# Sixth score buffer, a smaller pool of transposed weights, and another order of the last transposes in a top-k attention + MLP kernel

## The chip, the cores and the metric

The kernel runs on one core of a Trainium2 chip. The metric is the device time in microseconds (us) of one execution. A core has five engines that run their own instruction streams side by side: PE (matrix products), ACT (activation functions and copies), DVE (vector operations), POOL (vector operations too) and SP (here it only issues DMA transfers). Matrix products land in PSUM; the other engines work on SBUF and can read PSUM, POOL excepted in this kernel. Engines wait for each other through counting semaphores.

## The reference

Attention over 8 batches and 8 heads, 576 positions, head size 64, in which each query keeps only its 32 largest scores, followed by an MLP on the concatenated heads:

```python
scores = scale * q @ k.T
kth    = np.partition(scores, -32)[..., -32]      # the 32nd largest of each row
attn   = softmax(where(scores >= kth, scores, -1e9))
x      = (attn @ v) with the heads side by side    # 4608 x 512
h      = x @ w_in                                  # 4608 x 2048
out    = (maximum(h, 0) + alpha * minimum(h, 0)) @ w_out
```

The kernel folds the MLP's negative half into a linear product: with g = relu(h), the output is g @ ((1 - alpha) w_out) + x @ (w_in @ (alpha w_out)).

## The kernel before

Two heads form a pair, and the work is cut into 144 *duos*, 18 a batch. A duo is 128 query rows of both heads of a pair (or, for the 64 rows left over, the remainders of two pairs): two row blocks of 128 by 576 scores. D is the last duo, 143.

The main loop (`for n in range(ND)`) goes through 144 slots, and in each slot several duos are in work, each at another stage. In slot n:

- PE multiplies queries and keys of duo n+1 into PSUM (`st_qk`, tile `ps_sc`; there is one such PSUM tile), after waiting until the scores before were copied out.
- ACT counts for duo n-2 how many scores lie above an estimated threshold (`st_count`, tile `sg`, a sign with an accumulator), takes exp of the scores of duo n-4 (`st_exp`, tile `w`), writes its 0/1 mask with the final threshold (`st_cut`, tile `f`, two row blocks), and last copies the scores of duo n+1 from PSUM to SBUF (`st_exit`, tile `s_sb`). Every few slots it also copies transposed queries and keys (`qkT`) or output rows (`o_sb`).
- DVE takes the eight largest of each of six groups of every row of duo n (MAX8 from `s_sb`), folds them every second slot into a threshold estimate `p` that ACT's count of the next slots needs, picks the final threshold, takes MAX8 of `y`, and applies relu to MLP products (`gT`).
- POOL multiplies scores by signs (`st_y`, tile `y`) for duo n-2 and exp by mask (`w<-w,f`) for duo n-4.
- SP issues a DMA transpose of the masked weights of duo n-4 (`st_wT`, tile `wT`); PE multiplies `wT` with v (`st_av`, tile `xo`) in slot d+8 for duos d below 13 and in slot d+7 for the others. DVE normalizes every second duo to `x`, SP transposes x to `xT` (`st_xT`), and PE runs the MLP on it (`ph`: first layer, `pz`: second layer).
- Where PE would have nothing to do, products of a constant tile (`rest`) are put in.

The order on each engine is the order of the calls: the class `Ordered` keeps every engine's program order, apart from a group of small DVE operations. SP's queue is in order too: loads of q, k and v, transposes of `wT`, `x` and of the weights, copies into `kd`, and most output stores are issued in the order in which they are written, and a transfer that waits for its data holds those behind it.

Tiles come from pools with a fixed number of buffers. A new tile of a pool reuses the buffer that is oldest, and its first writer waits for the last reader of the tile that was there. In this program the wait stands also where reader and writer are on the same engine: each `st_exit` carries a wait for PE (the product) and one for ACT's own count (the last reader of the buffer). The pools of the change: `s` (5 buffers of 4608 bytes a partition, tile `s_sb`), tag `wT` of the pool `three` (4 buffers of 2560 bytes, given by `bufs=4`; the pool's own number is 3), and `qk` (6 buffers of 4608 bytes, tile `qkT`).

After the loop comes the *drain*, written out by hand: the last duos' counts, masks and products. For D-3 and D-2 `st_cut` makes the mask on ACT and POOL as before; for D-1 and D `st_mask` does it on DVE. The weights of D are transposed by PE (`turn_w`) and copied to SBUF by DVE and ACT (`turned`); those of the others by SP. `normed(D-4)` gives the `x` whose transpose feeds the last MLP block but one, `normed(D-2)` the last.

Of the kernel before, what the change touches and what calls it, by code (L numbers as in the profile page):

```python
# [9 lines left out]
BF16 = mybir.dt.bfloat16  # L10
# [49 lines left out]
def fast_path(tc, q, k, v, moe_w_in, moe_w_out, moe_alpha, out, flag):  # L60
    nc = tc.nc
    B, H, S, D = q.shape
# [26 lines left out]
    ND = len(duos)  # L89
# [3 lines left out]
    with ExitStack() as ctx:  # L93
        pool = lambda name, bufs, **kw: ctx.enter_context(tc.tile_pool(name=name, bufs=bufs, **kw))
# [1 line left out]
        stg = pool("stg", 3)  # L96
        io = pool("io", 2)
        qk_p = pool("qk", 2 * KPB - 2)
        s_p = pool("s", 5)
        two = pool("two", 2)  # L100
        three = pool("three", 3)
        gp = pool("gp", 4)
# [14 lines left out]
        qkT, v1 = {}, {}  # L117
# [114 lines left out]
        T = {}  # L232
# [162 lines left out]
        def st_cut(n):  # L395
            w, s = ws[n % 4][:, :, 0:S], T.pop(("s", n))
            f = two.tile([128, 2, S], mybir.dt.uint8, name="f", tag="sg", bufs=3)
            for i in range(2):
                ACT.activation(f[:, i, :], s[:, i, :], AF.Sign, bias=KT[:, 2 * n + i:2 * n + i + 1])
            POOL.tensor_tensor(w, w, f.bitcast(mybir.dt.float8e4), ALU.mult)  # L400
            st_wT(n)

        def st_wT(n):
            w = ws[n % 4]
            wt = three.tile([128, 10, 128], BF16, name="wT", tag="wT", bufs=4)
            SP.dma_start_transpose(wt, w.rearrange("p a b -> p (a b)"))
            T["wt", n] = wt

# [141 lines left out]
        def ready():  # L550
            k = 0
            while lin_done and k < len(oq) and oq[k][0]["done"] >= oq[k][1]:
                k += 1
            return k
# [16 lines left out]
        def o_pe():  # L571
            if ready() and len(stores) < (1 if now[0] < ND else 2):
                oq.pop(0)[2]()
                return True
# [160 lines left out]
        for n in range(ND):  # L735
# [33 lines left out]
            for m in duos_at("cut", n):  # L769
                st_cut(m)  # L770
# [26 lines left out]
        def st_mask(d):  # L797
            w, s_ = ws[d % 4], T.pop(("s", d))
            kt = KT[:, 2 * d:2 * d + 2]
            for i in range(2):  # L800
                DVE.scalar_tensor_tensor(out=w[:, i, 0:S], in0=s_[:, i, :], scalar=kt[:, i:i + 1],
                                         in1=w[:, i, 0:S], op0=ALU.is_ge, op1=ALU.mult)
            if d < D:
                st_wT(d)
# [6 lines left out]
            return ps  # L811

        def turned(d, ps):
            wt = T["wt", d] = three.tile([128, 10, 128], BF16, name="wT", tag="wT", bufs=4)
            DVE.tensor_copy(wt[:, 0:5, :], ps[0])
            ACT.copy(wt[:, 5:10, :], ps[1])

# [11 lines left out]
        D = ND - 1  # L829
# [18 lines left out]
        st_y(D)  # L848
        st_exp(D - 3)
        st_cut(D - 3)  # L850
        st_exp(D - 2)
        row(D - 1, 0)
# [10 lines left out]
        row(D, 0)  # L863
        row(D, 1)
        st_cut(D - 2)
        picked(D // 2)
        normed(D - 4)
# [7 lines left out]
        h_relu(ACT)  # L875
        st_mask(D - 1)
        st_mask(D)
        o_pe()
        o_pe()
        o_act()  # L880
# [4 lines left out]
        ps = turn_w(D)  # L885
        st_av(D - 3)
        turned(D, ps)
        h_pe(2)
        h_relu(ACT)
# [263 lines left out]
@with_exitstack  # L1153
def kernel(
    ctx: ExitStack,
    tc: tile.TileContext,
    q: bass.AP,
    k: bass.AP,
    v: bass.AP,
    moe_w_in: bass.AP,  # L1160
    moe_w_out: bass.AP,
    moe_alpha: bass.AP,
    out: bass.AP,
):
    nc = tc.nc
    keep = ctx.enter_context(tc.tile_pool(name="keep", bufs=1))
    flag = keep.tile([1, 1], I32, name="flag")
    fast_path(tc, q, k, v, moe_w_in, moe_w_out, moe_alpha, out, flag)
    redo = nc.values_load(flag, min_val=0, max_val=1)
    with tc.If(redo > 0):  # L1170
        general_path(tc, q, k, v, moe_w_in, moe_w_out, moe_alpha, out)
# [30 lines left out]
```

In the profile nearly all operations stand under L32, the line of the helper in `Ordered` that records them; tile names tell them apart.

## Time and profile before

| | |
|---|---|
| median of 3 runs | 824.95 us (823.41 to 827.95) |
| profiled execution | 827.92 us, span 826.0 us |
| clock of TensorE granted, mean | 0.988 |
| instructions | 17830 |
| busy PE / DVE / ACT / POOL | 738.5 / 757.0 / 778.8 / 715.6 us |
| share of the chain that ended last | ACT 47%, PE 35%, issue 9%, DVE 4% |

The span is the time from the first to the last instruction. Busy times are unions of instruction times on one engine, so two instructions that overlap count once. A row of a timeline gives start, length, engine, operation, output and input tiles, shapes and a count; in square brackets stands how long the engine was idle before, and what ended that. A row of the waits gives who waited for whom, the total in us, how often, and the longest. In a row of groups the part behind the second bar is idle time just before the instructions of the group. "SPq" is SP issuing a transfer; the time to landing runs from issue to the last byte.

### The profile page before, as it was taken

Reading aid. Unit: us, or ns where it says so; the run is one execution under the profiler, and the core shown is the slowest. Engines: PE = TensorE matmul, PEld = TensorE weight load, DVE = VectorE, ACT = ScalarE, POOL = GpSimd, SP = SyncE. Lnnn points to the kernel's source line nnn. Section 1 sums busy time; section 2 is a strip of 40 time slices with the busy share of each in tenths; the row PEclk is TensorE's granted clock in tenths of the full one; section 3 lists DMA queues with packets and bytes.
Section 4 is the critical chain, followed back from the end, with each engine's and each line's share of the span. In section 5 each row is a group of like instructions: output and inputs, shape, how many; then the busy total and the mean of one; then the engine's idle time right before and its main releaser. Section 6 shows DMA issues by size and latency. Waiting matters only on the chain.

```text
span 826.0 us, 17830 instructions
## 1 busy us (share of the span) xinstructions
PE 738.5 (89%) x5375; PEld 423.8 (51%) x5448; DVE 757.0 (92%) x3470; ACT 778.8 (94%) x1265; POOL 715.6 (87%) x565
## 2 busy tenths in 40 slices
PE   8878999989889988989989999898979999999876
PEld 5333455545545554555545554555545555556553
DVE  4999999999999999999999999999999999999841
ACT  5999999999999999999999999999999999999941
POOL 2898899999998999999999899999999988988930
PEclk9999899999999999999999999999999999999989
DMA  7789996555566565655676565666665564544441
GB/s 156 190 171 184 163 159 112 111 117 115 121 119 123 112 126 120 129 113 110 128 121 120 121 124 122 106 123 117 119 141 110 123 134 79 98 97 100 83 81 37
DMA packets 342327, 99.90 MB, mean 121 GB/s; under 512 B 336128, under 2 KB 336400, under 8 KB 342224
## 3 DMA queue, kind: packets, MB, share of 16 engines
q1 hardware_dynamic: 338928, 91.18, 57.0%
q0 software_dynamic: 1952, 7.09, 3.6%
q8 instruction: 45, 0.74, 0.4%
q10 hardware_dynamic: 1344, 0.43, 0.2%
q14 instruction: 58, 0.48, 0.2%
HBM read 36.71 MB, written 9.44 MB: 56 GB/s over the span
## 4 chain that ended last, share of the span: by engine, by line
ACT 47%; PE 35%; issue 9%; DVE 4%; POOL 2%; DMA 2%; SPq 1%; ACTq 0%; POOLq 0%; DVEq 0%
ACT f L32 14%; ACT sg L32 13%; PE ps_sc L32 12%; ACT s_sb L32 11%; ACT w L32 7%; PE pz L32 6%; PE ph L32 6%; PE xo L32 5%; PE rest L32 2%; PE tps L32 2%; DVE small L32 1%; PE plin L32 1%; ACT qkT L32 1%; SPq L32 1%; POOL w L32 1%
## 5 line engine op out<-in xcount | busy, mean ns | idle before, releaser
L32 POOL TENSOR_TENSOR y<-s_sb,sg 128x576 f32<-128x576 f32 x288 | 362.2, 1278 | 24.3 <-ACT sg L32 24.1
L32 POOL TENSOR_TENSOR w<-w,f 128x1152 bf16<-128x1152 bf16 x142 | 317.8, 2239 | 51.8 <-ACT f L32 47.3
L32 DVE MAX8 up<-s_sb 128x8 f32<-128x96 f32 x864 | 212.2, 246 | 18.0 <-ACT s_sb L32 17.5
L32 ACT ACTIVATE sg<-s_sb,p 128x576 bf16<-128x576 f32 x288 | 220.7, 770 | 2.1 <-DVE p L32 2.0
L32 DVE MAX8 p<-y 128x8 f32<-128x576 f32 x288 | 215.1, 748 | 7.2 <-POOL y L32 7.0
L32 DVE MAX8 small<-s_sb 128x8 f32<-128x96 f32 x864 | 216.2, 250 | 0.0
L32 PE MATMUL ps_sc<-qkT 64*128 64x512 f32 (+2 forms) x768 | 184.5, 570 | 26.0 <-ACT s_sb L32 25.1
L32 ACT ACTIVATE f<-s_sb,KZ 128x576 uint8<-128x576 f32 x284 | 203.0, 763 | 0.0
L32 ACT COPY s_sb<-ps_sc 128x1152 f32<-128x1152 f32 x144 | 161.1, 1118 | 9.5 <-PE ps_sc L32 5.1
L32 ACT ACTIVATE w<-s_sb 128x1152 bf16<-128x1152 f32 x144 | 166.2, 1154 | 0.0
L32 PE MATMUL ph<-xT,w_in_b 128*128 128x256 bf16 (+1 forms) x1472 | 151.2, 251 | 13.8 <-DMA xT<-x 7.2
L32 PEld LDWEIGHTS <-w_in_b 128*128 128x128 bf16 x1472 | 121.2, 99 | 56.8 <-issue 12.5
L32 PE MATMUL pz<-w_out_b,gT 128*128 128x512 bf16 x545 | 142.1, 379 | 8.9 <-issue 6.0
L32 PE MATMUL xo<-v,wT 128*128 128x65 bf16 (+3 forms) x1600 | 126.5, 198 | 0.6 <-DVE x L32 0.6
L32 PEld LDWEIGHTS <-wT 128*128 128x128 bf16 (+3 forms) x1600 | 97.7, 99 | 29.1 <-issue 0.8
L32 DVE TENSOR_SCALAR gT<-ph 128x512 bf16<-128x512 f32 x134 | 90.3, 674 | 8.3 <-PE ph L32 8.1
L32 PEld LDWEIGHTS ps_sc<-qkT 64*128 64x128 f32 (+1 forms) x768 | 55.7, 169 | 70.9 <-ACT s_sb L32 39.7
L32 PEld LDWEIGHTS ps_sc<-kd,qkT 128*128 128x128 f32 x256 | 38.3, 188 | 97.8 <-issue 94.8
L32 PEld LDWEIGHTS <-gT 128*128 128x128 bf16 x576 | 54.5, 98 | 59.0 <-issue 4.4
L32 PE MATMUL ps_sc<-kd,qkT 128*128 128x128 f32 x256 | 62.8, 327 | 0.0
L32 PE MATMUL rest<-idle 128*128 128x512 bf16 x200 | 52.2, 387 | 6.9 <-DVE gT L32 4.8
L32 ACT ACTIVATION_READ_ACCUMULATOR sg<-s_sb,p 128x1 f32 x288 | 54.8, 190 | 0.0
(67 smaller groups left out, 569.7 us busy)
## 6 DMA issues: line engine op xcount, KB each, us to landing
k_st<-in_k_dram SPq DMA_DIRECT2D x64, 128.0 KB, 2.9
v_st<-in_v_dram SPq DMA_DIRECT2D x64, 128.0 KB, 2.8
q_st<-in_q_dram SPq DMA_DIRECT2D x62, 128.0 KB, 2.7
out_dram<-o_sb SPq DMA_DIRECT2D x29, 256.0 KB, 2.5
w_st<-in_moe_w_out_dram POOLq DMA_DIRECT2D x4, 1024.0 KB, 6.7
wT<-w SPq DMA_TRANSPOSE x143, 3.5
w_in_b<-in_moe_w_in_dram POOLq DMA_DIRECT2D x4, 512.0 KB, 6.0
k_st<-in_k_dram SPq DMA_DIRECT2D x32, 32.0 KB, 2.8
```

The source lines that it names most:

```text
L32: ins = self.tc.keep_in_program_order(f(*a, **kw))
```

## The change

- The pool of scores has six buffers instead of five.
- The tag `wT` has three buffers instead of four.
- The transposed weights of the last duo, D, lie in a buffer of the pool of keys and queries instead of one of `wT`.
- `st_cut` of duo D-2 no longer issues the transpose of its weights; the drain issues it after `st_mask(D)`. On SP's queue it thereby stands behind the transpose of the x of D-4 and that of the weights of D-1, where it stood ahead of both.

The order of instructions on PE, ACT, DVE and POOL is the same as before.

```diff
-        s_p = pool("s", 5)
+        s_p = pool("s", 6)
...
         def st_cut(n):
...
             POOL.tensor_tensor(w, w, f.bitcast(mybir.dt.float8e4), ALU.mult)
-            st_wT(n)
+            if n < ND - 3:
+                st_wT(n)

         def st_wT(n):
             w = ws[n % 4]
-            wt = three.tile([128, 10, 128], BF16, name="wT", tag="wT", bufs=4)
+            wt = three.tile([128, 10, 128], BF16, name="wT", tag="wT")
             SP.dma_start_transpose(wt, w.rearrange("p a b -> p (a b)"))
...
         def turned(d, ps):
-            wt = T["wt", d] = three.tile([128, 10, 128], BF16, name="wT", tag="wT", bufs=4)
+            wt = T["wt", d] = qk_p.tile([128, 10, 128], BF16, name="wT", tag="qkT")
...
         st_mask(D - 1)
         st_mask(D)
+        st_wT(D - 2)
         o_pe()
```

## The prediction

> **What bounds the kernel now.** I read the busy shares first, then the stages.
>
> ```profile
> PE 738.5 (89%) x5375; PEld 423.8 (51%) x5448; DVE 757.0 (92%) x3470; ACT 778.8 (94%) x1265; POOL 715.6 (87%) x565
> ```
>
> ACT is the busiest engine. The table by stage (length, then busy us and instructions of PE, weight loads, DVE, ACT, POOL; clock; DMA) says where.
>
> ```profile
> 20.00:100.00 80.00, 66.74 (x360) 30.21 (x358) 75.24 (x332) 78.05 (x131) 72.12 (x65) 0.94 0.87 181
> 100.00:200.00 100.00, 92.43 (x642) 52.10 (x652) 94.57 (x439) 99.40 (x162) 91.97 (x69) 1.00 0.64 120
> 200.00:600.00 400.00, 360.94 (x2615) 207.66 (x2654) 389.44 (x1811) 397.43 (x641) 371.63 (x278) 1.00 0.62 121
> 600.00:700.00 100.00, 92.52 (x688) 54.17 (x697) 96.05 (x438) 97.14 (x157) 89.58 (x67) 1.00 0.60 118
> 700.00:775.00 75.00, 72.06 (x629) 43.31 (x638) 72.34 (x336) 74.00 (x121) 68.78 (x49) 1.00 0.46 90
> 775.00:826.00 51.00, 36.33 (x361) 25.12 (x365) 20.41 (x58) 21.26 (x37) 16.97 (x15) 0.90 0.35 68
> ```
>
> Through the loop of slots ACT is occupied 99.4% of the time, so ACT sets the period; DVE follows at 97.4%, two points behind. In the drain (after 775) no engine is full: there a chain of waits sets the end.
>
> **The sixth score buffer.** ACT's groups of 200 to 600 us (busy, mean ns | idle before):
>
> ```profile
> L32 ACT ACTIVATE f<-s_sb,KZ 128x576 uint8<-128x576 f32 x152 | 108.6, 763 | 0.0
> L32 ACT ACTIVATE w<-s_sb 128x1152 bf16<-128x1152 f32 x76 | 87.7, 1154 | 0.0
> L32 ACT COPY s_sb<-ps_sc 128x1152 f32<-128x1152 f32 x75 | 83.9, 1119 | 2.6 <-PE ps_sc L32 0.2
> ```
>
> Only the copy that brings scores out of PSUM has idle time before it: 2.6 us, of which PE explains 0.2; the other 2.4 over 75 copies is 0.032 us each. The timeline (start, length) shows its neighbours:
>
> ```profile
> 402.98 1.43 ACT L32 ACTIVATE f<-s_sb,KZ 128x576 uint8<-128x576 f32 x2
> 404.43 1.12 ACT L32 COPY s_sb<-ps_sc 128x1152 f32<-128x1152 f32 x1
> ...
> 770.12 0.19 ACT L32 ACTIVATION_READ_ACCUMULATOR sg<-s_sb,p 128x1 f32 x1
> 770.21 0.56 ACT L32 COPY o_sb<-pz 128x512 f32<-128x512 f32 x1
> ```
>
> Two masks `f` of 0.763 take 1.43, so they overlap by 0.096; and o_sb's copy, also out of PSUM, starts 0.10 before its predecessor (770.31) ends. The score copy alone starts 0.02 to 0.03 after `f` ends (404.41). With five buffers the copy of duo n+1 overwrites the scores of duo n-4, whose last reader is exactly the `f` ahead of it, and the program waits for that `f` by ACT's own count. With six it waits for the `f` of the slot before, five us old. I take the gap for that wait: each copy can start 0.032 + 0.096 = 0.128 us sooner. There are 75 copies in the 400 us, one every 5.33, so 19 in each 100 us and 14 in the 75; in the first stage, whose slots are longer, I put 13. So ACT could give back 1.7 + 2.4 + 9.6 + 2.4 + 1.8 = 17.9 us; nothing excludes 0 at the other end (the first rival).
>
> ACT is not alone, so I look at what is late next. Waits in 20:100, then 100:200, 200:600, 600:700 and 700:775 (total us, times, longest):
>
> ```profile
> DVE p L32 <- POOL y L32: 3.7, 8, 0.9
> DVE up L32 <- ACT s_sb L32: 1.0, 3, 0.3
> ...
> DVE up L32 <- ACT s_sb L32: 3.7, 6, 1.1
> ...
> DVE up L32 <- ACT s_sb L32: 6.9, 15, 0.7
> DVE p L32 <- POOL y L32: 0.7, 2, 0.3
> ...
> DVE gT L32 <- PE ph L32: 2.5, 4, 1.0
> ACT sg L32 <- DVE p L32: 1.4, 1, 1.4
> ...
> DVE up L32 <- ACT s_sb L32: 2.0, 4, 0.6
> ```
>
> Between 200 and 600 DVE waits 6.9 us for ACT's copy and 0.7 for POOL's products: 7.6, after which DVE is the bound. So 9.6 is cut to at most 7.6; I take 6.0 (6.9 less about one, since long and short slots alternate and ACT in turn needs DVE's thresholds). In 20:100 and 100:200 DVE's waits of 4.7 and more leave room: I take 1.4 of 1.7 and 2.0 of 2.4. In 600:700 DVE waits for PE, and ACT for DVE, never DVE for ACT: 0.5 of 2.4. In 700:775 1.5 of 1.8. Loop: 1.4 + 2.0 + 6.0 + 0.5 + 1.5 = 11.4, at most 1.7 + 2.4 + 7.6 + 2.4 + 1.8 = 15.9.
>
> The Trainium skill speaks against this in "VectorE: DVE Perf Modes", section "The DRAIN you can't avoid": for that engine it says of a wait between consecutive operations that "the semaphore costs nothing extra here". By it, carried over to ACT, the loop's term would be 0. The page measures another engine, and the copies above contradict it for ACT by 0.128 us each, unless something else makes that gap.
>
> **Three buffers for wT instead of four.** SP's transpose of duo d must now wait for the product with v of duo d-3, not d-4. Before duo 13 that product comes a slot later than the transpose:
>
> ```profile
> 86.66 1.75 SPq L32 DMA_TRANSPOSE wT<-w  x1
> 95.52 1.80 SPq L32 DMA_DIRECT2D q_st<-in_q_dram  x3
> ...
> 88.12 1.09 PE L32 MATMUL xo<-v,wT 128*128 128x65 bf16 x10
> 102.66 0.60 PE L32 MATMUL tps<-ident_f,q_st 128*128 128x128 f32 x4
> ...
> q_st<-in_q_dram SPq DMA_DIRECT2D x62, 128.0 KB, 2.7
> ```
>
> This is the worst of them: issued at 86.66, now held until 89.21, 2.55 later. Behind it SP is busy without a break, so the queries issued at 95.52 to 97.32 slip by 2.55 to 99.9 at most. They are used at 102.66, 2.8 after their last issue, where these transfers take 2.7 to land by their median (last row): cost 0, at most 0.5. If that cover were gone, the transposes of queries and then the next scores would wait up to 2.55 once. From duo 16 on the product with v is done before the transpose everywhere; the closest:
>
> ```profile
> 683.42 1.33 SPq L32 DMA_TRANSPOSE wT<-w  x1
> 681.65 0.78 PE L32 MATMUL xo<-v,wT 128*128 128x65 bf16 x10
> ```
>
> done 682.43, needed 683.42: 0.98 to spare. The last duo's wT in a buffer of keys and queries waits only for score products that ended slots before: 0.
>
> **The drain's order.** The transposes of D-2 move on SP's queue behind xT of D-4 and behind wT of D-1.
>
> ```profile
> 787.58 0.42 DVE L32 TENSOR_TENSOR x<-xo,KZ 128x256 bf16<-128x256 f32 x1
> 788.08 4.85 DVE L32 SCALAR_TENSOR_TENSOR w<-s_sb,KZ,w 128x576 bf16<-128x576 f32 x4
> ...
> 775.51 1.33 SPq L32 DMA_TRANSPOSE wT<-w  x1
> 776.90 1.38 SPq L32 DMA_TRANSPOSE xT<-x  x1
> ...
> 787.95 3.65 SPq L32 DMA_TRANSPOSE wT<-w  x2
> 791.66 1.99 SPq L32 DMA_TRANSPOSE xT<-x  x1
> ...
> 796.88 3.60 PE L32 MATMUL ph<-xT,w_in_b 128*128 128x128 bf16 x32 [5.25 <-DMA xT<-x]
> 805.57 0.78 PE L32 MATMUL xo<-v,wT 128*128 128x65 bf16 x10
> 809.53 1.95 PE L32 MATMUL ph<-xT,w_in_b 128*128 128x128 bf16 x32
> ...
> DMA to landing us min/median/max: 2.6/3.9/5.2
> ```
>
> x is ready at 788.00, but its xT is issued at 791.66, because wT of D-2 stands ahead and waits for POOL; PE then idles 5.25 us. Without it SP is free after wT of D-3, at 787.95 + 1.33 = 789.3: 2.3 earlier. Landing (last row) took 2.6 at 776.90, behind one transpose, and 5.2 at 791.66, behind two. Low end: 2.3 earlier with 5.2 again. High end: landing at 789.3 + 2.6 = 791.9, 4.9 earlier, and the matmuls at full pace (1.95 for 32, not 3.60 as after the idle stretch): 4.9 + 1.65 = 6.5. The new case resembles 776.90 ahead of it, 791.66 in what follows: 4.5.
>
> "TensorE: Matmul & The Clock Gate" of the Trainium skill ("What's actually happening") says that the clock is halved after an idle window of about 3.4 us. PE would idle from 791.63 for 0.3 to 2.9 us, so by it the 1.65 comes back at either end: 4.0 to 6.5. The trace agrees: 3.60 for 32 matmuls after 5.25 idle, and a granted clock of 0.90 in this stage.
>
> What is late next: wT of D-1 (mask done about 790.5) is issued near 790.8, wT of D-2 near 792.2, and may land near 798 even at 5.2. Its product with v, at 805.57 now, moves to about 800: 2 us of cover. Behind it on SP stands only the last xT, which depends on it anyway.
>
> **Sum.** Profiled execution: 827.92 - 11.4 - 4.5 = 812.0. It lies 3 us above the median of 824.95 and I subtract the same from that: 809.0. Half a per cent, about 4.1 us, is what a measurement of this kernel can tell from no change.
>
> **Rivals.**
> - *The gap is not the wait's.* If the 0.128 belongs to the copy itself (PSUM input after an SBUF input), the loop stays and the drain gives 2.3 to 6.5: 824.95 - 4.5 = 820.5. For it: every gap stands ahead of this one operation. Against it: o_sb's copy from PSUM overlaps. By the Trainium skill's "VectorE: DVE Perf Modes", carried over, it would end here.
> - *Nothing comes through.* The loop as above, and xT in the drain shares the transfers' time and lands as late as now: 825. Against it: the 2.6 at 776.90.
> - *SP is held, slower.* If products with v fall more than 0.98 us back against POOL's masks in later slots, as PE gets less slack per slot, SP's queue stands at every transpose, and the loads behind come late. PE waits for queries already:
>
> ```profile
> PE tps L32 <- DMA q_st<-in_q_dram: 3.8, 5, 1.3
> ```
>
> 0.76 each. If all 28 later pairs paid that, 21 us: 809.0 + 21 = 830. It decides from the point where PE's lag eats that margin; at 90% busy, filler products included, I doubt it.
>
> **How the numbers follow.** Forecast 0.74, first rival 0.13, second 0.04, third 0.09. Forecast's own range: 824.95 - 15.9 - 6.5 = 802.5 to 824.95 - 5.7 - 2.3 = 817 (half the loop). Taking in half of the first rival the range is 801 (the runs before spread 1.5 below their median) to 820.5; left out: 0.09 + 0.04 + 0.065, about 0.2. Faster by over 0.5%: 0.74 and half of 0.13, 0.80; within: the other half and 0.04, 0.11; slower 0.09.
>
> **What would show it.** The score copy's idle falls to near 0 and it starts about 0.1 before `f` ends; DVE rises above 98% between 200 and 600, with ACT waiting for thresholds; early wT issues come up to 2.5 later without a PE wait for queries; xT of D-4 is issued right after wT of D-3, and PE's idle ahead of its `ph` is under 3. I am wrong if the 0.03 gap stays, if PE or POOL take over as bound (more waits `p<-y` or `ps_sc`), or if PE waits for queries more than now.

## The result, and the profile after

The changed kernel takes 814.76 us (median of 4 runs, 814.29 to 815.29), the kernel before 826.42 in the runs beside it (823.41 to 827.95). The medians differ by 11.7 us; the ratio is put at 0.988, 95% interval 0.986 to 0.990, so 1.2% or about 10 us faster. The kernel before spreads over 4.5 us and the changed one over 1.0, so the difference depends on which executions of the kernel before it is taken from. Predicted were 809.0 in a range of 801 to 820.5. The profiled execution takes 814.44 us (before 827.92), its span is 812.4.

The stages of the profile after (length, then busy us and instructions of PE, weight loads, DVE, ACT, POOL; clock; DMA). The windows are those of the prediction; since the loop is shorter, the drain now begins at about 767.

```profile
20.00:100.00 80.00, 66.67 (x367) 30.47 (x367) 76.26 (x334) 78.43 (x134) 73.08 (x65) 0.96 0.95 182
100.00:200.00 100.00, 93.35 (x656) 52.81 (x664) 96.46 (x452) 98.97 (x163) 93.66 (x71) 1.00 0.65 124
200.00:600.00 400.00, 363.09 (x2630) 209.16 (x2667) 391.88 (x1826) 394.75 (x646) 372.90 (x280) 1.00 0.61 122
600.00:700.00 100.00, 93.76 (x698) 54.54 (x711) 95.96 (x442) 95.59 (x158) 90.12 (x68) 1.00 0.59 113
```

Between 200 and 600 us ACT fell from 397.43 busy to 394.75 and DVE rose from 389.44 to 391.88. Neither is full: 98.7% and 98.0%. ACT's groups in the same stretch (busy, mean ns | idle before), first the count's row in the kernel before, then the rows after and the timeline at one place:

```profile
L32 ACT ACTIVATE sg<-s_sb,p 128x576 bf16<-128x576 f32 x151 | 115.8, 770 | 0.0
...
L32 ACT ACTIVATE sg<-s_sb,p 128x576 bf16<-128x576 f32 x152 | 116.7, 770 | 5.1 <-DVE p L32 3.6
L32 ACT ACTIVATE f<-s_sb,KZ 128x576 uint8<-128x576 f32 x152 | 108.7, 765 | 0.0
L32 ACT ACTIVATE w<-s_sb 128x1152 bf16<-128x1152 f32 x76 | 87.8, 1155 | 0.0
L32 ACT COPY s_sb<-ps_sc 128x1152 f32<-128x1152 f32 x77 | 84.8, 1101 | 0.5 <-PE ps_sc L32 0.3
...
403.22 1.43 ACT L32 ACTIVATE f<-s_sb,KZ 128x576 uint8<-128x576 f32 x2
404.56 1.10 ACT L32 COPY s_sb<-ps_sc 128x1152 f32<-128x1152 f32 x1
```

The idle time ahead of the score copy is gone (2.6 to 0.5), and the copy starts 0.09 before the masks end (404.65). In its place stands idle time ahead of `sg`, the count, which had none: 5.1 us, of it 3.6 for DVE's threshold estimate p; the other 1.5 lies in stretches of under 0.15 us each, for which the profile names no cause. The waits in that stretch, of DVE and of ACT:

```profile
DVE up L32 <- ACT s_sb L32: 3.6, 13, 0.4
...
ACT sg L32 <- DVE p L32: 3.6, 12, 0.4
```

DVE's wait for the copy only halved (6.9 to 3.6), while ACT's wait for p came up from nothing. The loop's end is read from the last score copy, before and after:

```profile
773.20 1.12 ACT L32 COPY s_sb<-ps_sc 128x1152 f32<-128x1152 f32 x1
```

```profile
766.12 1.10 ACT L32 COPY s_sb<-ps_sc 128x1152 f32<-128x1152 f32 x1
```

It ends at 767.22 instead of 774.32: the loop gave 7.1 us. From there to the end of the span are 45.1 us instead of 51.6: the drain gave 6.5. SP and PE in the drain after:

```profile
773.48 8.72 SPq L32 DMA_TRANSPOSE wT<-w  x2
782.31 1.32 SPq L32 DMA_TRANSPOSE xT<-x  x1
784.53 3.92 SPq L32 DMA_TRANSPOSE wT<-w  x2
...
785.79 1.96 PE L32 MATMUL ph<-xT,w_in_b 128*128 128x128 bf16 x32 [1.14 <-DMA xT<-x]
792.11 0.78 PE L32 MATMUL xo<-v,wT 128*128 128x65 bf16 x10
...
DMA to landing us min/median/max: 3.4/3.4/3.4
```

xT of D-4 is issued right behind wT of D-3, lands 3.4 us later, and PE idles 1.14 us instead of 5.25. The 32 matmuls take 1.96 instead of 3.60.

### The profile page after: what moved, and what is told of

It is laid out like the page before. It is cut to its first block, busy times and chain, and to the rows that moved or that the text cites. A ratio compares the mean times of both kernels' runs of the same rounds, so it can differ in the third digit from the quotient of the medians.

```text
span 812.4 us, 17847 instructions
## 1 busy us (share of the span) xinstructions
PE 734.3 (90%) x5375; PEld 421.4 (52%) x5448; DVE 755.8 (93%) x3470; ACT 767.0 (94%) x1265; POOL 713.6 (88%) x565
## 4 chain that ended last, share of the span: by engine, by line
DVE 33%; PE 22%; ACT 18%; POOL 12%; issue 10%; SPq 2%; DMA 2%; ACTq 0%; POOLq 0%; DVEq 0%
DVE small L32 11%; PE ps_sc L32 7%; DVE p L32 7%; POOL y L32 7%; DVE up L32 6%; PE pz L32 5%; ACT f L32 5%; ACT sg L32 4%; ACT s_sb L32 4%; POOL w L32 4%; PE ph L32 4%; DVE gT L32 4%; PE xo L32 3%; ACT w L32 3%; SPq L32 2%
## 5 line engine op out<-in xcount | busy, mean ns | idle before, releaser
L32 ACT ACTIVATE sg<-s_sb,p 128x576 bf16<-128x576 f32 x288 | 221.6, 774 | 10.6 <-DVE p L32 8.3
L32 ACT COPY s_sb<-ps_sc 128x1152 f32<-128x1152 f32 x144 | 159.2, 1106 | 5.8 <-PE ps_sc L32 5.6
L32 PEld LDWEIGHTS ps_sc<-kd,qkT 128*128 128x128 f32 x256 | 38.1, 188 | 97.1 <-issue 93.3
```

What stands on the lines that cost most here:

```text
L32: ins = self.tc.keep_in_program_order(f(*a, **kw))
```

## Experiments

**The buffers without the reorder.** The change with `st_cut` and the drain as they were.

```diff
-            if n < ND - 3:
-                st_wT(n)
+            st_wT(n)
...
         st_mask(D)
-        st_wT(D - 2)
```

> The change without its reorder: six buffers of scores, three of wT, the last duo's wT in a buffer of keys and queries; the transpose of D-2 issued where it was. Theory (the gap ahead of the score copy is the wait for ACT's own mask, and the drain's gain is the reorder's alone): the idle time before s_sb that PE does not explain falls from 2.4 us per 400 to 0 and the copy starts 0.1 us before f ends; the last score copy ends about 7 us earlier than before (774.3 to about 767); the drain is as before, with PE idle 4 to 5 us before xT of D-4. Time: 7 us under the kernel before, ratio 0.991. Rival (the gap belongs to the copy from PSUM itself and the loop's gain came from elsewhere): gap 0.03 us, loop within 1 us of before, ratio 1.000.

820.88 us, ratio 0.9935 (0.9909 to 0.9961). The copy's row in the groups of 200 to 600 us, and PE's idle time in the drain:

```profile
L32 ACT COPY s_sb<-ps_sc 128x1152 f32<-128x1152 f32 x77 | 84.9, 1102 | 1.5 <-PE ps_sc L32 1.5
...
790.96 3.59 PE L32 MATMUL ph<-xT,w_in_b 128*128 128x128 bf16 x32 [5.65 <-DMA xT<-x]
```

What idle time the copy has left is PE's; the last copy ends at 767.9, 6.4 us earlier than before (7.1 with the change, about 7 expected); the drain is the old one (52.1 us). With the smaller pool alone, below, the loop gains nothing, so its gain is the sixth buffer's.

**The reorder alone**, with five and four buffers.

```diff
             POOL.tensor_tensor(w, w, f.bitcast(mybir.dt.float8e4), ALU.mult)
-            st_wT(n)
+            if n < ND - 3:
+                st_wT(n)
...
         st_mask(D)
+        st_wT(D - 2)
```

> The reorder of the drain's transposes alone, with five buffers of scores and four of wT. Theory: the loop is unchanged (last score copy ends at 774.3 within 0.5 us, gap before s_sb 0.03 us each), the drain is shorter by 6.5 us as in the changed kernel (2.3 from the earlier issue, the rest from a faster landing and from matmuls at full pace): ratio 0.992. Rival (the drain's gain needed the shifted loop or the other buffer of wT): 2.3 us or less, ratio 0.997 or more.

821.6 us, ratio 0.9957 (0.9940 to 0.9973). The same two rows:

```profile
L32 ACT COPY s_sb<-ps_sc 128x1152 f32<-128x1152 f32 x76 | 85.1, 1120 | 2.6 <-PE ps_sc L32 0.2
...
792.90 1.96 PE L32 MATMUL ph<-xT,w_in_b 128*128 128x128 bf16 x32 [0.19 <-DMA xT<-x]
```

The copy's gap is back (2.4 of 2.6 not PE's), the loop ends at 774.1, and the drain takes 45.4 us: 6.2 less than in the profiled execution before. Yet by the ratio the reorder is worth 3.5 us only; the further profiles of the kernel before, below, say why. The two parts multiply to 0.9892, close to 0.988.

**The smaller pool alone**: three buffers of `wT`, the last duo's in `qk`, all else as before.

```diff
-            wt = three.tile([128, 10, 128], BF16, name="wT", tag="wT", bufs=4)
+            wt = three.tile([128, 10, 128], BF16, name="wT", tag="wT")
...
-            wt = T["wt", d] = three.tile([128, 10, 128], BF16, name="wT", tag="wT", bufs=4)
+            wt = T["wt", d] = qk_p.tile([128, 10, 128], BF16, name="wT", tag="qkT")
```

> The smaller pool alone: three buffers of wT and the last duo's wT in a buffer of keys and queries, five buffers of scores, old order. Theory: the transposes of duos 3 to 15 are held by up to 2.6 us, hidden by their cover; cost 0 to 0.5 us, ratio 1.000. Rival (SP's queue, held, makes queries late): 2 to 20 us slower, ratio 1.002 to 1.025, with more PE waits for queries than 3.8 us.

825.56 us, ratio 1.0004 (0.9984 to 1.0024). PE's waits for queries are 3.9 us in all (3.8 before), and the loop ends within 0.3 us of before. The early transposes are issued up to 1.6 us later, and PE's waits hardly show it. This part gains no time; it gives back 2560 of the 4608 bytes a partition that a sixth score buffer takes. No run here has six score buffers and four of `wT`.

**ACT's count freed from DVE's p**, in the changed kernel.

```diff
-                ACT.activation(sg[:, i, :], s[:, i, :], AF.Sign, bias=p9[:, r, 0:1], scale=-1.0,
+                ACT.activation(sg[:, i, :], s[:, i, :], AF.Sign, bias=alpha1m[:, 0:1], scale=-1.0,
...
-            DVE.tensor_scalar(flag, lo1, 1e-30, None, ALU.is_le)
+            DVE.tensor_scalar(flag, lo1, -1e30, None, ALU.is_le)
```

> The changed kernel, with the count's threshold taken from a constant instead of DVE's estimate p, so ACT no longer waits for DVE (the counts, and so the weights and the output, are then not the reference's; the final check that would start the slow path is made to pass). Theory (the part of ACT's gain that did not come was lost because ACT, now earlier, waits for p, which delays its copy and then DVE in turn): ACT's wait for p, 8.3 us, goes to 0; DVE's wait for the score copy falls well under 10.9; the loop shortens by 3 to 6 us more, ratio 0.981 to 0.984 against before. Rival (POOL or PE became the bound): ACT's waits move to PE or POOL, loop within 1 us of the changed kernel, ratio 0.988.

805.29 us, ratio 0.9759 (0.9737 to 0.9782). Stage and waits between 200 and 600 us, and the last copy:

```profile
200.00:600.00 400.00, 365.14 (x2656) 211.07 (x2693) 395.19 (x1844) 398.08 (x656) 377.91 (x284) 1.00 0.63 123
...
ACT s_sb L32 <- PE ps_sc L32: 1.7, 4, 1.1
...
DVE up L32 <- ACT s_sb L32: 0.6, 1, 0.6
...
757.78 1.10 ACT L32 COPY s_sb<-ps_sc 128x1152 f32<-128x1152 f32 x1
```

ACT and DVE are both nearly full (99.5% and 98.8%), and the loop ends at 758.9, 15.4 us ahead of before, 8.3 more than with the change, where 3 to 6 were expected. So the part that did not come had gone into ACT's wait for p, and POOL and PE were not the bound. The run overstates that part: it also takes away the 2.0 us that ACT waited for p before the change.

**Making p earlier without changing what is computed.** In slots that make p, DVE's relu (first), its first MAX8 of `y` (second), or both (third) are issued behind p. The second:

```diff
                 negate()
+                least()
+                turn()
             else:
                 h_relu()
             for d in rows:
                 row(d, 0)
-            if turn:
-                least()
-                turn()
```

> The changed kernel, with DVE's relu of MLP products in odd slots issued behind the estimate p instead of ahead of it; p comes 0.6 us earlier, no work is added. Theory (what is left of the loop's gain is lost because ACT waits for p): ACT's wait for p falls from 8.3 us to under 2, the last score copy ends 3 to 8 us earlier than 767.2, ratio 0.978 to 0.984 against before. Rival (a later relu holds PE's next products, and PE passes the loss on): waits of PE for gT grow by more than 3 us and the loop is within 2 us of the changed kernel, ratio 0.986 to 0.990.

> The changed kernel, with the first MAX8 of y in odd slots issued behind p; p comes 0.7 us earlier and relu stays where it was. Theory as for the run with relu behind p: ACT's wait for p under 2 us, loop 3 to 8 us shorter, ratio 0.978 to 0.984. Rival (the short operations that make p, now back to back, each wait for the one ahead and cost DVE what ACT gains): DVE's small operations cost 0.1 us or more per odd slot, 7 us in all, loop within 2 us of the changed kernel.

> The changed kernel with both relu and the first MAX8 of y behind p in odd slots; p comes 1.3 us earlier. Theory: no more than the better of the two alone, within 1 us, since ACT's longest usual wait for p is 0.4 us; ratio 0.978 to 0.984. Rival (longer waits matter too): 2 us or more better than either alone.

With the row behind p: 810.75 us, ratio 0.9819 (0.9792 to 0.9845), faster than both kernels. With relu behind p: 819.76, 0.9917 (0.9889 to 0.9946). With both: 818.96, 0.9911 (0.9887 to 0.9935). First the row's kernel between 200 and 600, with its last copy:

```profile
200.00:600.00 400.00, 370.37 (x2683) 210.53 (x2682) 395.26 (x1834) 395.67 (x650) 374.93 (x282) 1.00 0.63 122
...
ACT s_sb L32 <- PE ps_sc L32: 1.9, 5, 0.9
ACT sg L32 <- DVE p L32: 1.9, 7, 0.3
...
762.61 1.10 ACT L32 COPY s_sb<-ps_sc 128x1152 f32<-128x1152 f32 x1
```

then relu's, over the whole span:

```profile
PE rest L32 <- ACT qkT L32: 15.0, 11, 1.7
...
PE pz L32 <- DVE gT L32: 10.3, 8, 1.9
...
ACT s_sb L32 <- PE ps_sc L32: 13.9, 17, 1.9
```

The row's MAX8 can wait: the loop ends at 763.7, 3.5 earlier than with the change, and ACT's wait for p falls from 3.6 to 1.9 in this stretch. Over the whole span it falls from 8.3 to 5.0, not to under 2 as expected. Relu cannot: ACT's wait for p falls to 6.9 only, PE waits for `gT` and for its PSUM buffers, gets to the next scores late, and ACT then waits 13.9 us for those scores (5.6 with the change). That is the rival, stronger than I had put it: the loop is worse than the change's by 6.0 us. The waits of ACT in the third, over the whole span:

```profile
ACT f L32 <- DVE KZ L32: 7.3, 19, 0.5
...
ACT sg L32 <- DVE p L32: 1.3, 2, 1.0
```

ACT hardly waits for p any more, but it now waits for the final threshold (`KZ`, also DVE's work) ahead of its masks, which it did not do in the changed kernel, and PE's waits for `gT` are 9.3 us, nearly those of the relu kernel. The loop ends at 772.1, 4.9 later than with the change. The third was expected within 1 us of the better of the other two and is 8 us behind it; since it pays for the relu too, it does not tell whether p earlier still would help.

**The drain's idle time filled**, in the kernel before, old order.

```diff
         o_act()
         o_sp()
+        for _ in range(5):
+            keep_warm()
```

> The kernel before with its old order in the drain, and five sets of products of a constant tile put where PE stands idle for 5.25 us ahead of the first layer on xT of D-4. Theory (part of the reorder's gain is that PE's clock is not lowered in that idle time, and its chance from run to run is what spreads the old order's times over 5 us): the 32 matmuls behind take 1.96 us and not 3.60, the times spread over less than 2 us, and the median lies at 822 to 824, near the fastest runs of before. Rival (the landing of xT varies and makes the spread): spread stays at 4 to 5 us, median within 0.5 us of before.

826.29 us, ratio 1.0008 (0.9991 to 1.0025), runs from 825.16 to 828.49. In the profiled execution:

```profile
792.86 4.48 PE L32 MATMUL rest<-idle 128*128 128x512 bf16 x20
797.18 1.95 PE L32 MATMUL ph<-xT,w_in_b 128*128 128x128 bf16 x32
```

The matmuls are at full pace, but the filling itself held PE until 797.2 in an execution where xT had landed earlier. The median did not fall, and the spread of 3.3 us lies between the under 2 of the theory and the 4 to 5 of the rival. The run says nothing clear about the spread.

**The kernel before, profiled three more times**, unchanged.

> The kernel before, unchanged, profiled again to find what differs between its short (823.4 to 824.3 us) and long (827 to 829 us) executions. If the landing of xT of D-4 makes the spread: in a short one PE's first layer starts 2 us or more earlier after the last score copy than the 22.6 us of the long one, at any clock. If the clock makes it: it starts at the same 22.6, and the 32 matmuls take about 1.96 us instead of 3.60. If neither, the loop's end moves by 3 us.

> The kernel before again, unchanged, for the same purpose: landing (first layer 2 us earlier after the last score copy), clock (same start, 32 matmuls in 1.96 us), or the loop (its end moved by 3 us).

> The kernel before a third time, unchanged, for the same purpose: landing (first layer 2 us earlier after the last score copy), clock (same start, 32 matmuls in 1.96 us), or the loop (its end moved by 3 us).

They took 823.36, 826.74 and 828.49 us. The first layer on xT of D-4 and xT's time to landing, in the first:

```profile
794.74 1.96 PE L32 MATMUL ph<-xT,w_in_b 128*128 128x128 bf16 x32 [2.10 <-DMA xT<-x]
...
DMA to landing us min/median/max: 3.5/3.5/3.5
```

and in the third:

```profile
798.69 3.50 PE L32 MATMUL ph<-xT,w_in_b 128*128 128x128 bf16 x32 [5.80 <-DMA xT<-x]
...
DMA to landing us min/median/max: 5.6/5.6/5.6
```

The second is like the third (5.3 to landing, idle 5.4, 3.59 for the matmuls). So landing and clock act together. The loop has a share too: its last copy ended at 773.9, 773.9 and 775.6. In the old order xT lands after 3.5 us, PE idles 2.1 and keeps its pace, and the drain takes 47.4 us; or it lands after 5.2 to 5.7, PE idles over 5, and the next 32 matmuls take 3.5 to 3.6: the drain takes 50.9 to 52.1. In the six traces with the new order it landed after 3.3 to 3.6. The reorder is thus worth 2.3 us against the first kind and 6.5 against the kind profiled for the prediction; 3.5, by the ratio above, is what it is worth over all runs. What decides between 3.5 and 5.2 in the old order is open.

## Why the prediction was right, and where not

*The gap ahead of the score copy is the wait's own.* Right. With six buffers the copy overlaps the masks by 0.10 (median), with five it follows them by 0.03, in every trace and whatever else is changed: 0.13 us a copy. The rival of a gap that belongs to copies from PSUM fell. That it is the wait, and not another effect of the sixth buffer, rests on the program's order of waits and on the copies of `o_sb`, which overlap; no run has five buffers without the wait. With the rival fell the carrying over to ACT of what the Trainium skill says of DVE ("VectorE: DVE Perf Modes", "The DRAIN you can't avoid"). The Trainium skill's own figure for ACT, in "ScalarE: Activation LUTs", section "What ACT_TABLE_LOAD costs", is that back-to-back ACTIVATEs overlap by about 93 ns; the trace agrees, with 0.10 for the copy behind the masks.

*The size of the loop's term.* This is the step that failed: "I take 6.0 (6.9 less about one ...)" for 200 to 600, and 11.4 in all. Measured are 7.1. By the ends of the same score copies (of duos 15, 34, 112, 130 and 143, near the stages' ends) the stages gave 1.7, 1.7, 3.1, 0.2 and 0.4 us, against 1.4, 2.0, 6.0, 0.5 and 1.5 foreseen. Room on DVE was counted as if ACT could use all of it. But p comes late in DVE's slot and ACT's next count waits for it; that delays ACT's copy at the slot's end, and DVE waits for the copy. I had named that exchange and taken about one microsecond off for it; the stage came out 2.9 lower still, and the other stages 1.4 lower together. The kernel with the row behind p, which computes the same, shows that the wait for p held the gain back: 200 to 600 gave 5.0 and its loop 10.6 in all. The kernel without the wait reached 15.4. That this is near the bound of 15.9 is in part luck: in 200 to 600 it gave 8.5, more than the 7.6 that I had called the most there, and in 600 to 700 only 0.5 of 2.4. The 99.4% of ACT that I read for the whole loop holds from 100 to 600 only; from 600 to 700 it was 97.1%.

*The smaller pool* costs nothing that shows, as said: ratio 1.0004 alone (0.9984 to 1.0024).

*The signs.* One of the signs of being wrong came: PE's wait for queries is 4.7 us instead of 3.8. It says little, since with five and four buffers it is 3.8 to 4.8 in the six traces there are. DVE between 200 and 600 came to 97.97%, just short of the 98% foreseen. ACT did wait for thresholds, and PE's idle time ahead of `ph` was under 3.

*The drain.* 4.5 between 2.3 and 6.5. It gave 6.5 against the profiled execution, 2.3 against a short one, both ends of the range. Of the 6.5 the earlier issue gave 2.3 us, as worked out. Landing took 3.4, between the rows of 2.6 and 5.2 that I used, and gave 1.7. The 32 matmuls gave 1.6, and the two groups of products behind them 0.8 more, which I had not counted: from 800.27 to 802.33 they took 2.06 us, after the change 1.27. That the whole meets the high end is thus partly luck. The transpose of D-2, which was moved back, landed at 791.42, 0.7 ahead of its product with v at 792.11; I had expected 2 us of cover. The granted clock was 0.50 over the 32 matmuls before (796.9 to 800.3) and 1.00 after; idle times of 1.1 and 2.1 us left the 32 matmuls at 1.96, 5.3 to 5.8 brought 3.5 to 3.6. This agrees with "TensorE: Matmul & The Clock Gate" of the Trainium skill ("What's actually happening", a window of about 3.4 us); no idle time ahead of them lies between 2.1 and 5.3, so the length of the window is not tested.

*The sum.* 809.0 is 5.8 below the measured 814.76. The loop's term makes 4.3 of it. The rest lies in the step from the profiled execution to the median of 824.95: seen from that median the drain gave 3.1 (824.95 - 7.1 - 814.76), not 4.5. The 3 us by which the profiled execution lay above the median were in the main its long drain (51.6 us, 47.4 in a short execution). The reorder removes them, and the changed kernel's profiled execution, 814.44, lies at its median. To take off both the 3 us and 4.5 for the drain counted part of the gain twice. The median is itself loose: with one run more it was 826.42.

## What to carry to other kernels

Where a pool's oldest buffer was last read by the instruction just ahead on the writer's engine, the writer waits for that instruction to end; here that cost ACT 0.13 us a copy, and one buffer more removed it. Look for a small constant idle time ahead of one group where all the others overlap. Where the next engine is within two per cent, do not count its room as gain: look which value each waits for from the other and how late in its slot that value is made, and issue it ahead of work that nobody waits for, here a MAX8 (3.5 us in the loop), but not relu, on which PE hung.

## What the runs showed of the hardware that I had not expected

The score copy itself became shorter once it no longer waited for the mask: 1.101 us on average between 200 and 600 instead of 1.119. It is 1.10 to 1.11 in every kernel with six buffers and 1.12 in every one with five; why is open. And the same transfer behind two transposes on SP's queue landed after either 3.5 to 3.6 or 5.2 to 5.7 us from one execution to the next; issued behind one, it took 3.3 to 3.6 in each of the traces.
